# One re-planned step order of a fused attention and feed-forward kernel: weights' mean in fp32 column quarters, factor table by products and two exponentials, tables held once, `w_in` in halves

## The chip, the core and the metric

The kernel runs on one core of a Trainium2 chip. A core has five engines with an instruction stream each: TensorE (PE, matrix products; its weight loads are listed as PEld), VectorE (DVE), ScalarE (ACT), GpSimd (POOL) and SyncE (SP, which here issues most of the DMAs). Every engine works through its own list in order; an instruction whose input is not there holds up all that stand behind it on that engine. The metric is the device time of one execution in microseconds (us). The kernel before takes 166.04 us (median of 2 runs, 165.97 to 166.11).

## The reference

Four batches of eight heads, 768 positions, 64 features. Attention keeps, for each query, the 96 latest keys and the first 8 keys of the sequence, with a bias that falls linearly with the distance. Its result, 3072 tokens by 512 features, goes through a feed-forward block.

```python
scores = scale * q @ k.T + bias                  # bias = -slope[head] * distance
keep = is_global | is_local                      # k < 8, or 0 <= q - k < 96
a = softmax(where(keep, scores, -1e9))
x = (a @ v) as [B*S, H*D]                        # 3072 x 512
h = x @ w_in                                     # 512 -> 1024
solu = h * softmax(h)
mu, var = mean(solu), var(solu)
out = ((solu - mu) / sqrt(var + 1e-6) * g_ln) @ w_out     # 1024 -> 512
```

## The kernel before, in words

**Attention.** Each batch is done in two units of 384 queries. For a unit, `q` and `k` are loaded with the positions in partitions, cast to fp16, turned by TensorE (six products of 128x128 with the identity per pair of heads, L729) and copied out of PSUM as `qT` and `kT` (L269 on ScalarE, L271 on VectorE; all casts and copies of those two engines go through one helper and so have one line). `scores` (L875) are products of key blocks with queries; ScalarE takes their exponential into `eb` (L883). The bias of batch 0 is added in PSUM by products with a table `bw` (L861); batches 1 to 3 take it as a factor, one VectorE multiplication of `eb` by a table `fb` per pair of heads and group (L891, the step `fac`, 24 of them). Column sums are products with ones (L954, L963); their reciprocals are made as exp(-log(sum)): `ln`, a split of the logarithm in two fp16 parts (`lhi` L977, `l` L985), a product that spreads them (L1014) and an exponential into `rr` (L1023). The weighted values are products in two parts: `av1`, then a VectorE copy of one column named `tick` (L1068), for which the second part `av2` waits (both L1058 and L1048). VectorE multiplies the result by `rr` into `xT` (L1083), the turned input of the feed-forward block.

**Feed-forward.** There are 24 tiles of 128 tokens, six to a batch. Per tile: gemm1 (L1117, 16 products of 128x512), an exponential `ef` on ScalarE (L1123), `uu` = h times ef on VectorE (L1126), squares and their sum on ScalarE (L1133) or VectorE (L1137), a turn of `uu` by TensorE or by DMA into `late`'s tiles, gemm2 (L1198, 8 products), and a scaling by the reciprocal deviation into `osb` on ScalarE (L1208) or VectorE (L1211), which is stored. The mean is not taken out of each token: gemm2's weights are centred once instead. The product with `g_ln` (L634, L636, L640) gives `gw_out_sb`, eight products with a matrix of 1/1024 (L647) give the mean over the 1024 rows in every partition, and eight VectorE instructions (L651, named centre here) write g times `w_out` less that mean.

**What sets the order.** All work is cut into some 760 steps. A planner outside the kernel chose the order, and the kernel holds its result as tables: ORDER (the steps' sequence), SLOTS (which buffer each takes), ENGS (the engine, where several could do it) and WARM (products on a constant tile, L1224, that are put in where TensorE would stand). Every engine's list follows from ORDER. The steps' priorities and costs, which the diff also touches, only fed that planner. At most eight loads or stores of SP are under way at a time.

## Time and profile before

| | |
|---|---|
| median of the runs | 166.04 us (165.97 to 166.11) |
| the profiled execution | 166.89 us, of which the span of the profile is 165.2 us |
| TensorE busy | 151.5 us (92%), of it 11.8 us in filler products |
| VectorE / ScalarE / GpSimd busy | 122.5 / 131.7 / 62.4 us |
| first gemm1 of batch 0 starts | 36.95 us |
| first gemm1 of batch 0's second unit starts | 55.37 us |
| first gemm1 of batch 2 starts | 112.64 us |
| last product ends | about 161.5 us |
| moved by DMA | 34.27 MB, mean 207 GB/s |

All times are counted from the span's start. Busy time is a sum over instructions; where it is near the length of a stretch, that engine has hardly stood in it. The profiled execution was 0.85 us longer than the median, so a sum made in its times has to be set against 166.89 us.

### The profile page before, as it was taken

Reading aid. Unit: us, or ns where it says so; the run is one execution under the profiler, and the core shown is the slowest. Engines: PE = TensorE matmul, PEld = TensorE weight load, DVE = VectorE, ACT = ScalarE, POOL = GpSimd, SP = SyncE. Lnnn points to the kernel's source line nnn. Section 1 sums busy time; section 2 is a strip of 40 time slices with the busy share of each in tenths; the row PEclk is TensorE's granted clock in tenths of the full one; section 3 lists DMA queues with packets and bytes.
Section 4 is the critical chain, followed back from the end, with each engine's and each line's share of the span. In section 5 each row is a group of like instructions: output and inputs, shape, how many; then the busy total and the mean of one; then the engine's idle time right before and its main releaser. Section 6 shows DMA issues by size and latency. Waiting matters only on the chain.

```text
span 165.2 us, 4904 instructions
## 1 busy us (share of the span) xinstructions
PE 151.5 (92%) x1936; PEld 83.6 (51%) x1936; DVE 122.5 (74%) x261; ACT 131.7 (80%) x217; POOL 62.4 (38%) x131
## 2 busy tenths in 40 slices
PE   6179988999999889989989999999999999999990
PEld 2046654545666556566545454465445564454550
DVE  6552657898976999997999999678687546758750
ACT  3279999999897987996989999599895775785901
POOL 7849642974312719940993436000205000000000
PEclk9999999999999999999999999999999999999997
DMA  4999999999999779999539999311349338429733
GB/s 146 275 378 293 344 386 322 330 308 321 310 307 278 199 171 294 368 256 248 181 77 211 214 193 210 128 72 63 64 88 122 124 62 201 108 76 108 200 130 129
DMA packets 57879, 34.27 MB, mean 207 GB/s; under 512 B 44920, under 2 KB 53376, under 8 KB 57856
## 3 DMA queue, kind: packets, MB, share of 16 engines
q1 hardware_dynamic: 56704, 31.99, 75.3%
q10 hardware_dynamic: 1152, 1.97, 3.2%
q8 instruction: 15, 0.25, 0.6%
q14 instruction: 8, 0.07, 0.1%
HBM read 23.20 MB, written 6.29 MB: 179 GB/s over the span
## 4 chain that ended last, share of the span: by engine, by line
PE 62%; DVE 13%; ACT 12%; issue 4%; DMA 3%; SPq 2%; POOL 2%; ACTq 0%; DVEq 0%
PE acc L1198 22%; PE acc L1117 20%; PE acc L1058 5%; PE acc L729 4%; ACT eb L883 4%; DVE eb L891 3%; DMA vgn<-in_v_dram 3%; DVE uu L1126 3%; PE acc L1224 3%; PE acc L1014 2%; DVE xT L1083 2%; PE acc L875 2%; ACT x L269 1%; PE acc L1152 1%; ACT gw_out_sb L634 1%
## 5 line engine op out<-in xcount | busy, mean ns | idle before, releaser
L1198 PE MATMUL acc<-gw_out_sb,late 128*128 128x512 f16 (+1 forms) x200 | 45.1, 371 | 0.1
L1117 PE MATMUL acc<-w_in_sb,xT 128*128 128x512 f16 x192 | 44.4, 379 | 0.6 <-DVE uu L1126 0.6
L1126 DVE SCALAR_TENSOR_TENSOR uu<-ef,acc 128x1024 f16<-128x1024 f16 x24 | 29.1, 1217 | 12.0 <-ACT ef L1123 11.7
L1123 ACT ACTIVATE ef<-acc 128x1024 f16<-128x1024 f32 x24 | 24.7, 1028 | 8.6 <-PE acc L1117 8.5
L883 ACT ACTIVATE eb<-acc 128x960 f16<-128x960 f32 (+1 forms) x32 | 29.1, 960 | 2.4 <-PE acc L875 2.4
L1117 PEld LDWEIGHTS <-xT 128*128 128x128 f16 x192 | 18.3, 98 | 21.3 <-issue 1.2
L1198 PEld LDWEIGHTS <-late 128*128 128x128 f16 x200 | 18.7, 98 | 20.1 <-issue 0.6
L729 PE MATMUL acc<-ident,x 128*128 128x128 f16 x192 | 16.5, 234 | 5.0 <-ACT x L269 4.1
L891 DVE TENSOR_TENSOR eb<-eb,fb 128x960 f16<-128x960 f16 (+1 forms) x24 | 18.3, 778 | 0.8 <-ACT eb L883 0.5
L1083 DVE TENSOR_TENSOR xT<-acc,rr 128x384 f16<-128x384 f32 x32 | 16.3, 552 | 2.8 <-ACT rr L1023 1.3
L273 POOL CAST x<-x 128x768 f16<-128x768 f32 x17 | 16.4, 979 | 5.1 <-DMA x<-in_q_dram 2.7
L1133 ACT ACTIVATE sqa<-uu 128x1024 f16<-128x1024 f16 x16 | 16.9, 1059 | 1.6 <-DVE uu L1126 1.5
L729 PEld LDWEIGHTS <-x 128*128 128x128 f16 x192 | 12.9, 104 | 10.3 <-ACT x L269 6.1
L977 POOL TENSOR_SCALAR lhi<-lns,mlo 128x384 f16<-128x384 f32 x5 | 7.1, 1411 | 27.1 <-ACT lns L970 27.1
L1058 PE MATMUL acc<-eb,v 64*64 64x160 f16 (+4 forms) x448 | 16.1, 220 | 0.4 <-DVE tick L1068 0.4
L1058 PEld LDWEIGHTS <-v 64*64 64x64 f16 x448 | 13.2, 106 | 4.4 <-issue 3.2
L1208 ACT ACTIVATE osb<-acc,rstd 128x512 f32<-128x512 f32 (+1 forms) x13 | 8.6, 669 | 7.3 <-PE acc L1198 5.8
L273 POOL CAST v<-v 128x704 f16<-128x704 f32 (+3 forms) x17 | 10.9, 656 | 8.7 <-DMA v<-in_v_dram 4.6
L1023 ACT ACTIVATE rr<-acc 128x768 f32<-128x768 f32 x16 | 12.8, 813 | 0.8 <-PE acc L1014 0.6
L1224 PE MATMUL acc<-busy 128*128 128x512 f16 x31 | 11.8, 494 | 1.5 <-DVE busy L554 1.5
L875 PE MATMUL acc<-qT,kT 64*64 64x160 f16 (+2 forms) x384 | 11.6, 230 | 0.6 <-ACT eb L883 0.5
L1211 DVE TENSOR_SCALAR osb<-acc,rstd 128x512 f32<-128x512 f32 (+1 forms) x12 | 8.7, 725 | 4.0 <-PE acc L1198 2.3
(115 smaller groups left out, 218.5 us busy)
## 6 DMA issues: line engine op xcount, KB each, us to landing
x<-in_q_dram SPq DMA_DIRECT2D x16, 384.0 KB, 5.2
x<-in_k_dram SPq DMA_DIRECT2D x16, 384.0 KB, 6.1
out_dram<-osb SPq DMA_DIRECT2D x16, 256.0 KB, 2.8
v<-in_v_dram SPq DMA_DIRECT2D x12, 192.0 KB, 4.8
w_out<-in_moe_w_out_dram SPq DMA_DIRECT2D x4, 512.0 KB, 6.3
late<-in_moe_w_in_dram SPq DMA_DIRECT2D x4, 512.0 KB, 6.8
v<-in_v_dram SPq DMA_DIRECT2D x12, 160.0 KB, 4.2
out_dram<-osb ACTq DMA_DIRECT2D x7, 256.0 KB, 2.9
```

The lines of the kernel that those rows point to most:

```text
L273: nc.gpsimd.tensor_copy(out=out, in_=in_)
L729: nc.tensor.transpose(out=pt[:, ts(j, P)], in_=a[:, j, ts(pp, P)], identity=ident)
L883: ex["fn"] = (lambda ex=ex, qk=qk, gw=gw: nc.scalar.activation(out=eb[at(qk, "eb")][:, :, 0:gw], in_=big(qk)[:, :, 0:gw], func=AF.Exp, sca ...
L891: nc.vector.tensor_tensor(out=e, in0=e, in1=fb[:, p, :, 0:gw], op=ALU.mult)
L1058: nc.tensor.matmul(out=o_[64 * h : 64 * h + 64, gl : gl + m], lhsT=vv[r, v_at(vi, h, c), pair, :], rhs=view(eb[at(e_own[b, gi, pair], "eb" ...
L1083: nc.vector.tensor_tensor(out=xT[at(xt_own[b], "xT")][:, p, q0:q1], in0=one(av, d)[:, 0:w], in1=rr[at(re, "rr")][:, d, 0:w], op=ALU.mult)
L1117: nc.tensor.matmul(out=ph()[:, ts(fh, 512)], lhsT=xT[at(xt_own[b], "xT")][:, j, ts(t % NA, P)], rhs=w_in_sb[:, j, ts(fh, 512)], start=(j = ...
L1123: ex["fn"] = lambda g1=g1, t=t, ph=ph: nc.scalar.activation(out=ef[at(g1, "ef")], in_=ph(), func=AF.Exp, accum_out=s0[:, t : t + 1])
L1126: u["fn"] = lambda u=u, g1=g1, t=t, ph=ph: nc.vector.scalar_tensor_tensor(out=uu[at(u, "uu")], in0=ef[at(g1, "ef")], scalar=USC, in1=ph(), ...
L1133: nc.scalar.activation(out=sqs_["ACT"], in_=uu[at(u, "uu")], func=AF.Square, accum_out=s2[:, t : t + 1])
L1198: nc.tensor.matmul(out=one(g2)[:, 0:wd], lhsT=uT[at(el_o, "uT")][:, c, :], rhs=gw_out_sb[:, c, sl_], start=(c == 0), stop=(c == NFC - 1))
L1224: nc.tensor.matmul(out=acc[:, spot, :], lhsT=busy16[:, 0:P], rhs=busy16, start=True, stop=True)
```

## The change

**The weights' mean.** The eight multiplications of `w_out` by `g_ln` (three on ScalarE, four on VectorE, one on GpSimd) are gone, and so are the eight fp16 products behind them. Instead `g` is copied 32 columns wide (`gbc`), and eight fp32 products of `gbc` with the loaded `w_out` write four column quarters of one bank, two of them adding up in each quarter (`part_mean`). ScalarE copies the bank to SBUF, and one fp32 product with a constant matrix of 1/32/1024 sums the quarters into the mean. The eight centre instructions stay.

**The factor table.** GpSimd's 16 memsets, its product over 128x1280, its copy over 128x2560 and ScalarE's exponential over 128x1280 are gone. Sixteen products of a 64x64 identity with `bw` put the bias into PSUM, and two exponentials write `fb` from there. Twelve memsets of GpSimd clear the last 32 columns of each `eb` buffer.

**Tables held once.** `bw` and `fb` are one window of 160 columns per pair instead of three side by side; products and `fac` read the window three times with a stride of zero. `fac` always works on 960 columns per partition, where it was 960 or 896.

**`w_in` in halves.** Its four loads were 128 rows of 1024 columns each; now each brings 256 rows of one half of the columns. gemm1 of the first six tiles is two steps, one per half.

**The plan.** ORDER, SLOTS, ENGS and WARM are new throughout. The buffers for loaded `q` and `k` go from six to seven, `uu` from three to four, `rr` from two to three. By the engine table, squares on VectorE go from 8 to 14 of 24, casts of `v` on VectorE from 3 to 6, fillers from 31 to 24.

```diff
 ORDER = """
-11 12 2 161 614 65 139 31 10 6 13 73 3 105 18 123 7 25 4 14 66 16 1 19 86 24 47 0 75 92 5 112 76
+11 12 10 112 139 65 281 19 105 118 2 120 157 7 13 47 0 92 5 295 114 79 15 1 115 14 107 16 25 6 17
...
 WARM = """
-32:0:7 54:0:3 60:0:1 66:0:3 93:4:1 124:2:4 142:4:3 177:5:2 189:5:3 194:5:2 199:7:1 203:7:1
+24:0:5 47:2:0 76:4:1 115:4:1 131:0:6 153:6:3 186:0:1 197:0:5 232:0:1 299:2:1
...
+    def factor_bias(s, d):
+        for par in range(2):
+            for n in range(2):
+                p = 2 * d + n
+                for h in range(2):
+                    o, r = 64 * (h ^ par), slice(64 * h, 64 * h + 64)
+                    nc.tensor.matmul(
+                        out=big(s)[o : o + 64, par, n * WIN : (n + 1) * WIN], lhsT=identb[r, r],
+                        rhs=bw[r, p], start=(n == 0), stop=(n == 1), tile_position=(64 * h, o),
+                        skip_group_check=True)
+
+    def factor_exp(s, d):
+        nc.scalar.activation(
+            out=fb[:, 2 * d : 2 * d + 2].rearrange("r p x n -> r x p n"),
+            in_=big(s)[:, :, 0 : 2 * WIN].rearrange("r x (p n) -> r x p n", n=WIN), func=AF.Exp, scale=inv_sqrt_d)
...
-        for j in range(NCC):
-            _, d = load(lambda i, e, j=j: e.dma_start(
-                out=w32[:, j], in_=moe_w_in.rearrange("(j p) f -> p j f", p=P)[:, j]),
...
+        for fh in range(2):
+            for jj in range(0, NCC, 2):
+                _, d = load(lambda i, e, jj=jj, fh=fh: e.dma_start(
+                    out=w32[:, jj : jj + 2, ts(fh, 512)],
+                    in_=moe_w_in.rearrange("(j p) f -> p j f", p=P)[:, jj : jj + 2, ts(fh, 512)]),
...
-        def mean():
+        pm = step("PE", 1750, 24000, w_out_st + [gb], None, take="one", mode="s", name="part_mean", lat=210, ni=16)
+
+        def parts():
             for j in range(NFC):
-                nc.tensor.matmul(out=one(hold), lhsT=onesm, rhs=gw_out_sb[:, j, :],
-                                 start=(j == 0), stop=(j == NFC - 1))
...
+                x = 32 * (j % 4)
+                nc.tensor.matmul(out=one(pm)[x : x + 32], lhsT=gbc[:, j], rhs=w_out32[:, j],
+                                 start=(j < 4), stop=(j >= 4), tile_position=(0, x), skip_group_check=True)
+        pm["fn"] = parts
+        pc = step(("ACT", "DVE"), (530, 610), 24500, [pm], None, free=[(pm, "one")], lat=(165, 140), name="copy_mean")
+        pc["fn"] = lambda: copy(pc["at"], part, one(pm))
+        wm = step("PE", 870, 25000, [pc, onesm_st, hold], lambda: nc.tensor.matmul(
+            out=one(hold), lhsT=onesq, rhs=part, start=True, stop=True), mode="f", name="mean", lat=210, ni=2)
...
                     def factor(qk=qk, gw=gw, p=p):
-                        e = eb[at(qk, "eb")][:, :, 0:gw]
-                        nc.vector.tensor_tensor(out=e, in0=e, in1=fb[:, p, :, 0:gw], op=ALU.mult)
+                        e = eb[at(qk, "eb")].rearrange("r x (m n) -> r x m n", n=WIN)
+                        f = fb[:, p]
+                        nc.vector.tensor_tensor(
+                            out=e, in0=e, in1=bass.AP(tensor=f.tensor, offset=f.offset,
+                                                      ap=[f.ap[0], f.ap[1], [0, 3], f.ap[2]]),
+                            op=ALU.mult)
...
-        g1 = step("PE", 1728, tt, xt_st[t] + w_in_st, None, take=("big", "ef"), mode="f",
-                  name="gemm1", lat=198, ni=16)
...
+        g1 = step("PE", 864 if early else 1728, tt, xt_st[t] + (w_in_st[:NCC] if early else w_in_st), None,
+                  take=("big", "ef"), mode="f", name="gemm1", lat=198, ni=8 if early else 16)
+        g1e = g1
+        if early:
+            g1e = step("PE", 864, tt + 900, [g1] + w_in_st[NCC:], None, mode="f", name="gemm1b", lat=198, ni=8)
```

What the new tables move is shown at three places. In the changed kernel the lines are L602 for `w_in`'s loads, L613 for `w_out`'s, L634 for centre, L871 for `fac`, L1066 for `xT`, L1117 for `uu`, L1128 for squares, L1202 for `osb`, L1051 for `tick` and L273 for VectorE's casts and copies.

The first place is SP's list around `w_in` and the last loads of `w_out`; `x` are loads of `q` and `k`. Before:

```order
L621 DMA w_out_70<-in_moe_w_out_dram 128x2x512 x2
L611 DMA late<-in_moe_w_in_dram 128x1024
L481 DMA x_5_105<-in_q_dram 128x2x384
L495 DMA v_0_110<-in_v_dram 128x3x64 x2
L503 DMA vt_88<-in_v_dram 64x4x64
L510 DMA vgn<-in_v_dram 64x1x64
L611 DMA late<-in_moe_w_in_dram 128x1024 x3
```

Of the change:

```order
L602 DMA late<-in_moe_w_in_dram 128x2x512
L485 DMA v_2_115<-in_v_dram 128x3x64
L485 DMA v_2_115<-in_v_dram 128x2x64
L613 DMA w_out_72<-in_moe_w_out_dram 128x2x512
L602 DMA late<-in_moe_w_in_dram 128x2x512 x3
```

The last load of `w_out` has moved behind the first of `w_in`. Of the four loads of `w_in`, the two with the second half of the columns stand first, and the two with the first half, for which gemm1's first step waits, come last.

The second place is VectorE's list from the first `xT` to the `xT` of batch 0's second unit. Before, five of the centre instructions stand ahead of the first `xT`, and these rows lead on from the last two of the eight:

```order
L891 TENSOR_TENSOR eb_139<-eb_139,fb 128x2x448
L891 TENSOR_TENSOR eb_140<-eb_140,fb 128x960
L1126 SCALAR_TENSOR_TENSOR uu_150,s_92<-ef_148,acc 128x1024
L271 COPY kT_118<-acc 128x768
L1126 SCALAR_TENSOR_TENSOR uu_151,s_92<-ef_149,acc 128x1024
L271 CAST x_3_109<-x_2_102 128x768
```

Of the change:

```order
L1066 TENSOR_TENSOR xT_100<-acc,rr_150 128x384 x2
L871 TENSOR_TENSOR eb_141<-eb_141,fb 128x960
L273 CAST w_in_sb<-late 128x512
L634 SCALAR_TENSOR_TENSOR gw_out_sb<-w_out_72,g_74,acc 128x512 x8
L1117 SCALAR_TENSOR_TENSOR uu_154,s_94<-ef_152,acc 128x1024
L871 TENSOR_TENSOR eb_142<-eb_142,fb 128x960
L1128 SCALAR_TENSOR_TENSOR sqv,s_95<-uu_154 128x1024
L1117 SCALAR_TENSOR_TENSOR uu_155,s_94<-ef_153,acc 128x1024
```

All eight centre instructions now stand in one piece behind the first unit's `xT` and ahead of the first `uu`, and a square that ScalarE did has joined VectorE's list. From the first centre to the second unit's last `xT`, VectorE's list holds: the 8 centres, 3 `uu`, 2 squares, 2 `fac`, one copy each of `qT`, `kT` and `late`, two small casts of `v`, the four rows of a statistics group, one `osb`, 2 `tick` and 4 `xT`.

The third place is VectorE's list between the second unit's `xT` and the first `xT` of batch 2, at its start. Before:

```order
L271 CAST x_3_109<-x_2_102 128x768
L891 TENSOR_TENSOR eb_131<-eb_131,fb 128x960
L271 CAST v_1_114<-v_0_110 128x11x64
L891 TENSOR_TENSOR eb_133<-eb_133,fb 128x960
L891 TENSOR_TENSOR eb_134<-eb_134,fb 128x2x448
L891 TENSOR_TENSOR eb_132<-eb_132,fb 128x2x448
L1126 SCALAR_TENSOR_TENSOR uu_150,s_92<-ef_149,acc 128x1024
```

Of the change:

```order
L273 CAST x_2_111<-x_5_107 128x768
L273 CAST x_3_112<-x_2_104 128x768
L273 CAST x_0_109<-x_1_103 128x768
L871 TENSOR_TENSOR eb_136<-eb_136,fb 128x960
L871 TENSOR_TENSOR eb_135<-eb_135,fb 128x960
L273 COPY qT_127<-acc 128x768
L871 TENSOR_TENSOR eb_133<-eb_133,fb 128x960
L273 COPY qT_125<-acc 128x768
L1117 SCALAR_TENSOR_TENSOR uu_157,s_94<-ef_153,acc 128x1024
```

Two casts and two copies have come in ahead of the first `uu`, and one `fac` has gone. Over the whole stretch the list holds, before and with the change: `fac` 15 and 12, squares 5 and 7, casts of `x` 3 and 5, casts of `v` 1 and 3, copies of `qT` and `kT` 4 and 5, `lhi` 2 and 1, `l` 2 and 1, `osb` 1 and 3, statistics groups 3 and 2; 12 `xT`, 9 `uu`, 6 `tick` and one copy of `late` in both. TensorE's list holds, between that first `xT` of batch 2 and batch 2's first gemm1, one gemm2, one product group of L1014 and one turning of `q` fewer than before, and two scores more; behind that gemm1 it holds the same groups as before, 12 gemm1 and 13 gemm2 among them.

157 lines of the change are left out of this document (62 added, 95 removed), and 93 rows, old and new, of tables (ENGS, ORDER, SLOTS).

## The prediction

> **What bounds the kernel now.** First the page's busy times, to see which engine could set the span at all.
>
> ```profile
> span 165.2 us, 4904 instructions
> PE 151.5 (92%) x1936; PEld 83.6 (51%) x1936; DVE 122.5 (74%) x261; ACT 131.7 (80%) x217; POOL 62.4 (38%) x131
> ```
>
> An average of 92% hides stages with different limits. So the span is cut where the dependences cut it: at the first gemm1 (36.95), the first gemm1 of batch 0's second unit (55.37), the first of batch 1 (79.68), the first of batch 2 (112.64) and the end of the products. The columns are the stretch's length, then busy time and instructions of PE, PEld, DVE, ACT and POOL, the granted clock, the DMA share and GB/s.
>
> ```profile
> 0.00:36.95 36.95, 29.79 (x424) 16.35 (x425) 23.52 (x67) 29.08 (x40) 24.72 (x82) 1.00 1.01 309
> 36.95:55.37 18.42, 17.88 (x252) 11.04 (x251) 14.82 (x30) 16.85 (x30) 5.67 (x13) 1.00 1.05 302
> 55.37:79.68 24.31, 23.02 (x392) 14.28 (x389) 22.86 (x42) 21.30 (x34) 14.14 (x18) 1.00 0.95 253
> 79.68:112.64 32.96, 32.02 (x471) 17.61 (x467) 29.38 (x56) 29.59 (x50) 14.42 (x17) 1.00 0.74 161
> 112.64:161.50 48.86, 48.82 (x412) 24.36 (x408) 31.93 (x71) 34.37 (x66) 3.41 (x3) 1.00 0.53 110
> ```
>
> From 112.64 TensorE stands for 0.04 us in all: whatever delays batch 2's first gemm1 delays the end by as much, and nothing behind it matters. In 36.95 to 112.64 TensorE stands for 75.69 − 72.92 (the three rows' sum) = 2.77 us: that is all a better order can win there. The first 36.95 us are not TensorE's own, though it looks busy; the fillers alone (line L1224) show it:
>
> ```profile
> 0.00:36.95 36.95, 11.63 (x31) 3.21 (x31) 1.00 1.01 309
> ```
>
> Useful there are 29.79 − 11.63 = 18.2 us. The DMA engines are full, and ScalarE ends the wait: the last cast of `w_in` on it ends as the first gemm1 starts.
>
> ```profile
> 36.28 0.61 ACT L269 CAST w_in_sb<-late 128x512 f16<-128x512 f32 x1
> ```
>
> The engine to watch behind that is VectorE. From the `xT` of batch 0's second unit to the first `xT` of batch 2:
>
> ```profile
> 52.91:103.19 50.28, 47.56 (x737) 27.86 (x728) 47.74 (x87) 45.31 (x75) 29.31 (x35) 1.00 0.93 220
> ```
>
> It is busy 47.74 of 50.28 us, 95%, and the chain that ended last runs through it there:
>
> ```profile
> 57.43 2.24 DVE eb L891 x3
> 59.67 1.15 DVE uu L1126 x2
> ```
>
> It has 2.5 us to spare in 50. A plan that gives it more work there has to find the room.
>
> **The change part by part.** The sum is made from the profiled execution's span, whose execution took 166.89 us, 0.85 above the median of 166.04; a difference found in it is set on the median.
>
> *Repeated tables.* `fac` now reads `fb` three times over. The nearest row is VectorE's own repeated read, 1280 columns in 483 ns, against the present `fac`:
>
> ```profile
> L271 DVE COPY bw<-bw 128x1280 f16<-128x1280 f16 x1 | 0.5, 483 | 0.0
> L891 DVE TENSOR_TENSOR eb<-eb,fb x24: 610/651/1459, 27.8 to 114.3; 128x960 f16<-128x960 f16 x12, 128x896 f16<-128x896 f16 x12
> L1083 DVE TENSOR_TENSOR xT<-acc,rr x32: 546/550/559, 33.8 to 137.7; 128x384 f16<-128x384 f32 x32
> ```
>
> The repeat cost that copy no pace, so I take none for `fac`; above, its slow value, 1459. That spread, beside `xT`'s 2%, means `fac` is stretched by something else. By the Trainium skill, "SBUF — State Buffer", section "SBUF: two separate sides", a GpSimd instruction and a VectorE one with two SBUF inputs shut each other out; `fac` (two) against `xT` (one) agrees with it. By that rule GpSimd's lost table work would help only where `fac` runs, and it went from the head.
>
> *Weights' mean.* These go, or are replaced:
>
> ```profile
> L647 PE MATMUL acc<-gw_out_sb,onesm 128*128 128x512 f16 x8 | 1.9, 379 | 0.0
> L640 DVE TENSOR_SCALAR gw_out_sb<-w_out,g 128x512 f16<-128x512 f32 x4 | 2.8, 739 | 0.6 <-DMA w_out<-in_moe_w_out_dram 0.6
> L634 ACT ACTIVATE gw_out_sb<-w_out,g 128x512 f16<-128x512 f32 x3 | 2.1, 733 | 0.8 <-DMA vgn<-in_v_dram 0.8
> L651 DVE SCALAR_TENSOR_TENSOR gw_out_sb<-w_out,g,acc 128x512 f16<-128x512 f32 x8 | 5.6, 742 | 0.5 <-PE acc L647 0.5
> ```
>
> VectorE loses 2.8 and ScalarE 2.1 us, ahead of the first gemm1. No trace here shows an fp32 product of this size. Below, four quarters could run beside each other like the four 32-column products of L927, whose group is hardly longer than one of them:
>
> ```profile
> 23.84 0.35 PE L927 MATMUL acc<-qT,kg 128*32 128x384 f16 x4
> L927 PE MATMUL acc<-qT,kg 128*32 128x384 f16 x32 | 2.6, 335 | 0.6 <-DVE kT L271 0.6
> 37.12 3.45 PE acc L1117 x16
> ```
>
> At the fp16 pace of gemm1, 3.45 / 16 = 0.216 us a product, two rounds would take 0.43. Above: fp32 numbers taken as two halves make four products of each, and eight in a row take, as an estimate from that pace, 8 × 4 × 0.216 = 6.9. I take quarters side by side with four products each, 2 × 4 × 0.216 = 1.75, and 4 × 0.216 = 0.87 for the last product. The Trainium skill, "FP8 and Floating Point Precision", section "TensorE Precision Notes", counts four passes for true FP32, and "TensorEngine Tiling (Array Packing)", section "Key Properties", lets different tiles work in parallel but says that a change of tiling mode drains TensorE; L927 bears out the parallel tiles, no run here shows the passes, and by these rules the two steps give the same 1.75 and 0.87 plus two drains of unknown length.
>
> The mean's products stood ahead of the first spread (L1014) before; now they stand behind `av2`, whose last row is the first here, and the copy through ScalarE follows:
>
> ```profile
> 33.83 0.45 PE L1058 MATMUL acc<-eb,v 64*64 64x160 f16 x7
> 30.02 2.72 DVE L651 SCALAR_TENSOR_TENSOR gw_out_sb<-w_out,g,acc 128x512 f16<-128x512 f32 x4 [0.46 <-PE acc L647]
> 52.91 1.95 DVE L1083 TENSOR_TENSOR xT<-acc,rr 128x384 f16<-128x384 f32 x4 [0.54 <-PE acc L1058]
> ```
>
> If `av2` ends where it did, at 34.3, the centres can start at 34.3 + 1.75 + 0.7 + 0.9 = 37.6; if the 2.1 us off ScalarE and the mean's 1.9 out of spread's way pull it forward in full, at 33.6. I take 36.0, past the middle, because more bytes lie ahead (below); before, the first started at 30.02 and five were done ahead of the first `xT`. VectorE's prices, from its groups between 52.91 and 103.19:
>
> ```profile
> L1126 DVE SCALAR_TENSOR_TENSOR uu<-ef,acc 128x1024 f16<-128x1024 f16 x9 | 10.8, 1213 | 0.4 <-issue 0.3 <-ACT ef L1123 0.2
> L1137 DVE SCALAR_TENSOR_TENSOR sqv<-uu 128x1024 f16<-128x1024 f16 x5 | 6.7, 1350 | 0.1
> L891 DVE TENSOR_TENSOR eb<-eb,fb 128x960 f16<-128x960 f16 x7 | 6.5, 935 | 0.1
> L891 DVE TENSOR_TENSOR eb<-eb,fb 128x896 f16<-128x896 f16 x8 | 6.2, 785 | 0.1
> L271 DVE COPY kT<-acc 128x768 f16<-128x768 f16 x4 | 3.7, 954 | 0.3 <-POOL v L273 0.3
> L271 DVE CAST x<-x 128x768 f16<-128x768 f32 x3 | 2.4, 797 | 0.0
> L977 DVE TENSOR_SCALAR lhi<-lns,mlo 128x384 f16<-128x384 f32 x2 | 1.3, 666 | 0.0
> L985 DVE TENSOR_TENSOR l<-lns,lhi 128x384 f16<-128x384 f32 x2 | 1.1, 546 | 0.0
> L271 DVE CAST v<-v 128x704 f16<-128x704 f32 x1 | 0.9, 875 | 0.0
> L1172 DVE SCALAR_TENSOR_TENSOR va<-s,va 128x3 f32<-128x3 f32 x3 | 1.1, 355 | 0.2
> L1211 DVE TENSOR_SCALAR osb<-acc,rstd 128x512 f32<-128x512 f32 x1 | 0.7, 736 | 0.0
> ```
>
> From 36.0 VectorE has, in a row: 8 centres at 2.72 / 4 = 0.68, 5.4; 3 `uu` at 1.21, 3.6; 2 squares at 1.35, 2.7; 2 `fac` at 0.65, 1.3; three copies at 0.95, 0.95 and 0.68, 2.6; casts of `v` 0.35; a statistics group of four rows up to 0.36, 0.9; `osb` 0.75; ticks 0.3; 4 `xT` 1.95. That is 19.9, and ends at 55.9 where it ended at 52.91 + 1.95 = 54.86: **+1.0** (−1.4 to +2.6) at the second unit. ScalarE's gain is swallowed there, since `uu` stands behind all eight centres.
>
> *`w_in` in halves, loads.* The half that gemm1's first step needs lands last, so splitting gives nothing by itself. Ahead of the last `w_in` load stand 10196 KB instead of 9732, counted from the two lists by the page's sizes: 464 KB, 1.5 us at the 309 GB/s of the first window. The same bytes in `w_out`'s shape land sooner:
>
> ```profile
> w_out<-in_moe_w_out_dram SPq DMA_DIRECT2D x4, 512.0 KB, 6.3
> late<-in_moe_w_in_dram SPq DMA_DIRECT2D x4, 512.0 KB, 6.8
> ```
>
> Between 0 and 0.5 each comes off, up to 2.0; I take the two as even. ScalarE then casts up to 0.7 sooner, which counts only in the rival below.
>
> *Factor table.* GpSimd loses these two, and ScalarE an exponential of 1.3, for two exponentials of about 0.6:
>
> ```profile
> L316 POOL TENSOR_TENSOR fx<-dm,sf 128x1280 f32<-128x1280 f32 x1 | 2.3, 2318 | 0.0
> L328 POOL COPY fb<-fb 128x2560 f16<-128x2560 f16 x1 | 2.3, 2317 | 0.1
> ```
>
> Nobody waited for them, and the new small products (about 0.4) replace fillers in the first 10 us: 0 to −0.5, taken as 0. The cover is the loads; without it the 0.4 would count.
>
> *The stretch 52.91 to 103.19.* By the prices above and the counts shown with the change: squares +2 with their readout, 2.9; casts of `x` +2, 1.6; of `v` +2, 1.75; a copy, 0.95; `osb` +2, 1.5; `lhi`, `l` and a statistics group less, −0.7 − 0.55 − 0.9; `fac` from 12.7 to 12 of 0.85 to 0.935, −2.5 to −1.5. That is +4.0 to +5.0: 51.7 to 52.7 us of work in a stretch of 50.28. It takes 51.7 if VectorE never stands and 52.7 / 0.95 = 55.5 if it stands as now. I take 52.2 / 0.975 = 53.6: **+3.3** (+1.5 to +5.2). Against it, between that `xT` and batch 2's gemm1 TensorE has one gemm2 (1.73) less, and L1014 and a turning less against two more scores come out even: **−1.7**. Behind that gemm1 the work is the same.
>
> The sum: 1.0 + 3.3 − 1.7 = +2.6, the profiled 166.89 to 169.5, the median to **168.6**; from the ends, −1.4 + 1.5 − 1.7 and 2.6 + 5.2 − 1.7, 164.4 to 172.1.
>
> **The rivals.** *VectorE keeps up.* TensorE alone binds, gemm1 starts up to 0.7 sooner by ScalarE's relief, and of the 2.77 us of standing some goes: 166.04 − 0.7 − 0.7 = 164.6, at most −0.7 − 2.77, 162.6. For it speaks that four `uu` and three `rr` buffers loosen the order; against it the 95%.
>
> *The fp32 quarters run one after the other.* Slower: `part_mean` takes 6.9, 5.1 more, and the centres start at 41.1; VectorE's list has no room until the second unit's gemm1, so all of it lands: 173.7. It decides once the quarters' end passes the landing of `w_in`, some 2 us above the value taken. The parallel L927 speaks against it.
>
> *The repeat costs `fac` its pace.* At twice 0.65, 12 in the stretch and 2 ahead: 14 × 0.65 = 9.1 less the spare 1.3, 176. The copy of `bw` speaks against it.
>
> *The change does not do what it says* in one part: the halves of `w_in`, counted above at nothing.
>
> **How the numbers follow.** VectorE takes over 0.55 (164.4 to 172.1; 0.30 of it below 169.4), VectorE keeps up 0.29, quarters in a row 0.10, `fac` loses pace 0.06. A measurement of this kernel can tell about 2% from no change, 162.7 to 169.4. Faster: 0.05, from the second case's best end. Same: 0.30 + 0.24 = 0.54. Slower: 0.25 + 0.10 + 0.06 = 0.41. The range, 163.6 to 172.6, leaves out the quarters' and `fac`'s cases and the second case's best end, about 0.2.
>
> **What would show it.** Right: the second unit's first gemm1 at 56 to 57, VectorE over 97% busy from there to batch 2's first `xT`, TensorE standing 4 to 6 us between its first and 13th gemm1 where it was 2.77, `part_mean` near 1.75. Wrong: the 13th gemm1 before 112.6, `fac` far under 0.78 in the mean since less of GpSimd runs beside it, or `av` so early that the centres start at 33.

## The result

The changed kernel takes 171.85 us (median of 2 runs, 170.98 and 172.73) against 166.04: 1.033 times the time before (95% interval 1.028 to 1.039), **slower by 5.8 us**. The prediction said 168.6 in a range of 163.6 to 172.6: the measured time is inside it and on the forecast side of no change, but the forecast has less than half of the loss, and it held "same" (0.54) likelier than "slower" (0.41). A run more than 1.5% above the fastest of the same kernel is left out of the ratios below, so the kernel with `w_in`'s loads in another order, of whose four runs one remains, has none.

The page of the changed kernel, busy times (profiled execution 172.73 us, the longer of its two runs, against 166.89 before):

```profile
span 170.7 us, 4929 instructions
PE 154.7 (91%) x1955; PEld 84.0 (49%) x1955; DVE 131.6 (77%) x275; ACT 125.0 (73%) x206; POOL 53.7 (31%) x116
```

The span of the changed kernel, cut at the same five events (columns as in the prediction):

```profile
0.00:37.54 37.54, 30.23 (x422) 16.99 (x422) 23.91 (x64) 27.07 (x38) 16.64 (x73) 0.95 0.96 301
37.54:57.44 19.90, 18.69 (x253) 10.52 (x252) 17.61 (x36) 15.38 (x27) 7.10 (x9) 1.00 1.00 280
57.44:85.69 28.25, 24.91 (x442) 15.30 (x434) 25.57 (x43) 23.71 (x37) 17.65 (x22) 1.00 0.94 245
85.69:118.34 32.65, 32.09 (x447) 17.10 (x441) 31.61 (x65) 25.41 (x43) 7.59 (x10) 1.00 0.67 135
118.34:167.33 48.99, 48.80 (x408) 24.09 (x407) 32.92 (x72) 32.98 (x63) 4.69 (x4) 1.00 0.53 116
```

Held against the rows before, the five stretches are longer by 0.6, 1.5, 3.9, −0.3 and 0.1 us. So 5.7 of the 5.84 us are there when the 13th gemm1 starts (118.34 for 112.64), and two thirds arose between the second unit's first gemm1 and that of batch 1. That stage does not hold quite the same work: TensorE has 442 products in it instead of 392, 44 of the 50 more being scores, and is busy 1.9 us longer, while the stage behind it holds 24 fewer. Between the first gemm1 and the 13th TensorE is busy 75.69 us instead of 72.92 (+2.8) and stands 5.1 us instead of 2.8 (+2.3). In what follows, "the stretch" without more is this one: 75.7 us before, 80.8 after.

Where it shows is the chain of waits. Before, from the product of L1014 that spreads the first logarithms of batch 1 to that batch's `xT`:

```profile
73.95 0.36 PE acc L1014 x4
...
74.66 1.83 PE acc L1198 x8
...
76.83 0.16 PE acc L1014 x4
...
78.78 0.71 ACT rr L1023
...
79.52 0.56 DVE xT L1083
```

And after, the same place (the spread is L997, gemm2 L1189, `osb` on ScalarE L1199):

```profile
74.94 0.38 PE acc L997 x4
...
77.59 2.61 DMA out_dram<-osb
80.20 0.68 ACT osb L1199
80.88 2.10 ACT rr L1006 x3
...
83.85 0.40 DVE xT L1066
```

The first of these spreads is only 1.0 us late (74.94 for 73.95). From there to batch 1's first gemm1 it takes 79.68 − 73.95 = 5.7 us before and 85.69 − 74.94 = 10.8 after. TensorE's timeline of the changed kernel has two gemm2 between the first spread and the others where one stood before, and ScalarE's has an `osb` that waits for a store to free its buffer ahead of three `rr`:

```profile
76.53 3.63 PE L1189 MATMUL acc<-gw_out_sb,late 128*128 128x512 f16 x16
80.08 0.52 PE L997 MATMUL acc<-l,onesr 64*64 64x384 f16 x8
```

```profile
80.19 0.69 ACT L1199 ACTIVATE osb<-acc,rstd 128x512 f32<-128x512 f32 x1 [0.99 <-DMA out_dram<-osb]
80.78 2.20 ACT L1006 ACTIVATE rr<-acc 128x768 f32<-128x768 f32 x3
```

### The profile page after: what moved, and what is told of

The parts are those of the page before. It is cut to its first block, busy times and chain, and to the rows that moved or that the text cites. A ratio compares the mean times of both kernels' runs of the same rounds, so it can differ in the third digit from the quotient of the medians.

```text
span 170.7 us, 4929 instructions
## 1 busy us (share of the span) xinstructions
PE 154.7 (91%) x1955; PEld 84.0 (49%) x1955; DVE 131.6 (77%) x275; ACT 125.0 (73%) x206; POOL 53.7 (31%) x116
## 4 chain that ended last, share of the span: by engine, by line
PE 49%; DMA 15%; ACT 12%; DVE 10%; SPq 4%; POOL 4%; issue 3%; POOLq 0%; ACTq 0%; DVEq 0%
PE acc L1189 21%; PE acc L1104 17%; DMA late<-in_moe_w_in_dram 5%; DMA v<-in_v_dram 5%; DMA x<-in_q_dram 4%; ACT eb L862 4%; PE acc L1041 3%; SPq L471 2%; DVE eb L871 2%; ACT ef L1114 2%; ACT rr L1006 2%; PE acc L712 2%; DVE x L273 2%; DMA out_dram<-osb 2%; PE acc L854 2%
## 5 line engine op out<-in xcount | busy, mean ns | idle before, releaser
L1104 PE MATMUL acc<-w_in_sb,xT 128*128 128x512 f16 x192 | 45.3, 379 | 1.5 <-DVE uu L1117 0.7
L1189 PE MATMUL acc<-gw_out_sb,late 128*128 128x512 f16 (+1 forms) x200 | 44.5, 371 | 0.0
L1117 DVE SCALAR_TENSOR_TENSOR uu<-ef,acc 128x1024 f16<-128x1024 f16 x24 | 29.1, 1215 | 6.9 <-ACT ef L1114 6.8
L862 ACT ACTIVATE eb<-acc 128x896 f16<-128x896 f32 (+1 forms) x32 | 29.3, 951 | 3.0 <-PE acc L854 2.9
L1189 PEld LDWEIGHTS <-late 128*128 128x128 f16 x200 | 18.7, 98 | 21.1 <-DMA late<-uu 0.5
L712 PE MATMUL acc<-ident,x 128*128 128x128 f16 x192 | 17.7, 240 | 2.9 <-POOL x L275 1.2
L1066 DVE TENSOR_TENSOR xT<-acc,rr 128x384 f16<-128x384 f32 x32 | 16.4, 550 | 3.0 <-ACT rr L1006 1.9
L1128 DVE SCALAR_TENSOR_TENSOR sqv<-uu 128x1024 f16<-128x1024 f16 x14 | 17.8, 1268 | 0.1
L871 DVE TENSOR_TENSOR eb<-eb,fb 128x960 f16<-128x960 f16 x24 | 17.3, 735 | 0.6 <-ACT eb L862 0.6
L275 POOL CAST x<-x 128x768 f16<-128x768 f32 x14 | 12.6, 901 | 13.4 <-DMA x<-in_q_dram 6.6
L1199 ACT ACTIVATE osb<-acc,rstd 128x512 f32<-128x512 f32 (+1 forms) x14 | 9.1, 654 | 7.2 <-PE acc L1189 4.8
L854 PE MATMUL acc<-qT,kT 64*64 64x160 f16 (+2 forms) x384 | 13.7, 237 | 0.7 <-ACT rr L1006 0.3
L271 ACT CAST x<-x 128x768 f16<-128x768 f32 x9 | 7.5, 837 | 5.2 <-DMA x<-in_k_dram 3.2
L1124 ACT ACTIVATE sqa<-uu 128x1024 f16<-128x1024 f16 x10 | 10.5, 1052 | 0.9 <-DVE uu L1117 0.9
L854 PEld LDWEIGHTS <-kT 64*64 64x64 f16 x384 | 9.6, 111 | 3.1 <-issue 2.0
```

Of the source, the lines that this page charges most:

```text
L712: nc.tensor.transpose(out=pt[:, ts(j, P)], in_=a[:, j, ts(pp, P)], identity=ident)
L854: nc.tensor.matmul(out=sc[o : o + 64, par, col : col + n], lhsT=kk[r, BLK * c : BLK * c + BLK], rhs=qq[r, g0 : g0 + n], start=fresh, stop= ...
L862: ex["fn"] = (lambda ex=ex, qk=qk, gw=gw: nc.scalar.activation(out=eb[at(qk, "eb")][:, :, 0:gw], in_=big(qk)[:, :, 0:gw], func=AF.Exp, sca ...
L871: nc.vector.tensor_tensor(out=e, in0=e, in1=bass.AP(tensor=f.tensor, offset=f.offset, ap=[f.ap[0], f.ap[1], [0, 3], f.ap[2]]), op=ALU.mult)
L1066: nc.vector.tensor_tensor(out=xT[at(xt_own[b], "xT")][:, p, q0:q1], in0=one(av, d)[:, 0:w], in1=rr[at(re, "rr")][:, d, 0:w], op=ALU.mult)
L1104: nc.tensor.matmul(out=ph()[:, ts(fh, 512)], lhsT=xT[at(xt_own[b], "xT")][:, j, ts(t % NA, P)], rhs=w_in_sb[:, j, ts(fh, 512)], start=(j = ...
```

## The experiments

The edits of the tables are given by the steps that they move, since the rows of numbers tell nothing. `u` is the step of `uu`, `sq` a square; a number behind `#` names the step of its kind. The "stretch" figures are from each kernel's own profile, cut at the same events.

### The parts without the new order

Two kernels with the order and engines of before: one with all four parts of the change, one with all but the new mean.

```diff
 # order, engines and buffers of before; the code of the changed kernel
-gw#0..7, mean (8 fp16 products)
+part_mean, copy_mean (ScalarE), mean (fp32), in the old mean's place
+c_fbias#0..1 and c_fac#0..1 among the first turns
```

> All four parts of the change (mean in fp32 quarters, factor table by products, tables held once, w_in in halves with the first half loaded first), but the order, the engine of each step and the buffers as the kernel before has them. Theory O, that the new order and engine table cost the 5.8 us and the parts cost nothing: 164.5 to 167 us. Theory P, that the parts themselves cost (the fp32 mean comes late, the halves and the repeated tables cost TensorE and VectorE time): 169 us or more.

> Three parts of the change (factor table by products and two exponentials, tables held once, w_in in halves) with the mean, the order and the engines of the kernel before. If the 3.5 to 4.4 us by which the first gemm1 came late in the two runs of all parts were the mean's longer path, as their traces say (ScalarE or TensorE stood for the quarters): first gemm1 at 36.5 to 37.5 and 165 to 167 us. If the repeated tables, the halves or the small products cost something too: 168 us or more.

All four parts: 169.85 us, 1.021 (1.013 to 1.028). Without the mean: 168.2 us, 1.012 (1.006 to 1.019). The stretch takes 75.3 and 75.9 us, as before (75.7), and the loss lies ahead of it: the first gemm1 starts at 40.41 and 39.68 instead of 36.95 (the second figure from that kernel's longest run, 169.61, with a granted clock of 0.87 in the head). So **behind the first gemm1 the parts cost nothing in these two kernels**, the table read three times among them. In the head they cost here what the forecast gave no price for. Two of TensorE's waits in the head of the kernel with all parts:

```profile
PE acc L997 <- ACT eb L862: 2.2, 1, 2.2
...
PE acc L712 <- ACT fb L320: 0.8, 1, 0.8
```

The kernel before has neither of the two; its wait for the casts of `x`, 4.1 us in all, is as long there as here and no part of the loss. ScalarE is late by then: it holds the table's two exponentials, and it stood 1.6 us for the quarters' products before it could copy them. Since in these two kernels the places in the head are mine, two other placings were tried.

```diff
 # the same parts and the old order, first other placing
-turn_k#4, part_mean; copy_mean on ScalarE; four centres ahead of tick, the others among and behind the xT
+part_mean, turn_k#4; copy_mean on VectorE; one centre ahead of tick, 7 in one piece behind the last xT
```

> All four parts again in the order and with the engines of the kernel before, with the new steps placed so that nothing stands for them: the copy of the quarters on VectorE, where it has room, the products of the factor table ahead of two exponentials that take the place of two multiplications by g on ScalarE, seven of the centres behind the first unit's xT. Theory O (order costs, parts are free): the first gemm1 back at 36.5 to 37.5 where parts_old_order had 40.4, the stages behind it as long as before, 165 to 167 us. Theory P: the first gemm1 at 38.5 or later, or longer stages, 168 us or more.

```diff
 # second other placing
+turn_k#4, part_mean, ..., turn_q#4, mean; copy_mean on VectorE; 5 centres behind the last xT, 2 behind the first u
```

> All four parts in the order and with the engines of the kernel before, once more with other places in the first 37 us: the products of the factor table in a bank that no filler waits for, the quarters' copy on VectorE behind the first unit's logarithm, the fp32 sum of the quarters behind the next turning, five centres behind the first unit's xT and two behind the first uu. In parts_old_order, parts_old_order2 and old_mean_old_order the stages behind the first gemm1 were as long as before to 0.4 us (but for the second's first stage), and only the head was longer. If it was my places there: first gemm1 at 36.5 to 38 and 165 to 167 us. If the parts cost the head something wherever they stand: 39 or later, 168 us or more.

171.64 us, 1.034 (1.029 to 1.038), and 169.62 us, 1.017 (1.012 to 1.022). In the first the head takes 41.33 us and the stretch 76.7, since the first `uu` stands behind the seven centres. In the second the head takes 38.06 and the stretch 78.0: TensorE stands behind the first gemm1, for a bank that the mean holds until the last centre has read it, and for `uu`:

```profile
PE acc L712 <- DVE gw_out_sb L634: 1.9, 1, 1.9
PE acc L1143 <- DVE uu L1117: 0.5, 1, 0.5
```

In three placings the parts cost 2.8 to 5.6 us in the old order (0.017 and 0.034 of 166.04). None was free, but all three are my own places in a finished order, so whether the parts have a price of their own in the head stays open. What is shown is that the table's products and exponentials and the mean's longer path find no slack there by themselves. The stage from the second unit's first gemm1 to batch 1's takes 23.5 to 24.3 us in all four of these kernels, as before (24.31). The stage ahead of it, 18.4 in the first two as before, takes 20.2 and 20.8 in the two that have seven centres behind the first unit's `xT`; the change has all eight there and 19.9.

### VectorE's load

Does the work that the new table gives VectorE explain the stretch? Once in the old order, by giving VectorE as many squares as the change does:

```diff
 # the kernel before; ENGS
-sq#1, 3, 11, 6, 8, 14: ScalarE
+sq#1, 3, 11, 6, 8, 14: VectorE
```

> The kernel before with six more squares on VectorE (14 of 24, as the change has), its order unchanged; 7.8 us come on VectorE, five of the six between its first gemm1 and batch 2's, and 7.5 us go off ScalarE. Theory V: VectorE's 2.5 us of room there are used up, so 168 to 170 us. Theory W: 165.5 to 167.5 us.

172.34 us, 1.039 (1.034 to 1.044): **in the old order six squares alone cost as much as the whole change**. VectorE's busy time in the stretch goes from 67.1 to 73.2 us and the stretch from 75.7 to 80.5; the change takes VectorE to 74.8 and the stretch to 80.8. Its longest stage, from batch 1's first gemm1 to batch 2's, took 35.33 us instead of 32.96:

```profile
82.61:117.94 35.33, 32.46 (x470) 17.73 (x467) 32.87 (x62) 26.93 (x44) 14.98 (x17) 1.00 0.70 155
```

VectorE does 32.87 us of work there, where it did 29.38, and TensorE stands for 2.9 us where it stood for 0.9.

Then in the new order, by taking work off VectorE:

```diff
 # the changed kernel; ENGS
-sq#0, 2, 3, 6, 8, 11: VectorE
+sq#0, 2, 3, 6, 8, 11: ScalarE
```

> The changed kernel with six of its fourteen squares on VectorE given back to ScalarE (8 on VectorE as before), the order unchanged. Theory V, that VectorE's list is what binds between the first gemm1 and batch 2's first: two squares of 1.3 us go ahead of the second unit's xT and three or four behind it, so 167.5 to 170 us. Rival theory W, that waits of TensorE on several engines, set by the order, cost the time whoever does the squares: 171 to 174 us, since ScalarE gets 6 times 1.25 us more.

```diff
 # the changed kernel; ENGS
-cast_q#11, 12, 14, 15, cast_k#10, cast_v#14, 17, 19: VectorE
+cast_q#11, 12, 14, 15, cast_k#10, cast_v#14, 17, 19: GpSimd
```

> The changed kernel with five casts of q and k and three of v given from VectorE to GpSimd, which is busy for 17.7 of 28.3 and 7.6 of 32.7 us in the two stages; 6.7 us go off VectorE between the second unit's xT and batch 2's, and none comes on ScalarE. Theory V (VectorE's load binds, 25.6 of 28.3 and 31.6 of 32.7 us busy): 167.5 to 169.5 us. Theory W (the order's waits cost the time whoever does the work): 171 to 173 us.

Both together:

> The changed kernel with both six squares on ScalarE and eight casts on GpSimd: 14 us off VectorE, which then has as little to do as before. If VectorE's load is what the new order loses by (as it is for the old order with six more squares, 172.3 us): 166 to 169 us. If the new order loses by its own waits and by what it adds on TensorE (75.7 us busy against 72.9 between the first gemm1 and batch 2's): 170 us or more.

172.67 us, 1.037 (1.029 to 1.045); 170.97 us, 1.028 (1.020 to 1.036); 172.97 us, 1.034 (1.025 to 1.043). VectorE's busy time in the stretch falls to 66.3, 69.1 and 62.5 us, below that of before in two of the three, and the stretch stays at 80.5, 80.1 and 82.2 (the last with a granted clock of 0.92 in its first stage). The squares bring ScalarE to 70.2 us there, above the 67.7 of before; the casts leave it at 64.3. With the casts on GpSimd, the stage from the second unit's first gemm1 to batch 1's:

```profile
56.06:83.59 27.53, 24.14 (x443) 15.02 (x435) 21.45 (x40) 23.18 (x37) 19.26 (x24) 1.00 1.01 258
```

VectorE works 21.45 us in it, less than before (22.86), and the stage takes 27.53 us instead of 24.31. So more work on VectorE is enough to cost 5 us, but it is not what holds the new order: once relieved, it waits for the others. The reading "VectorE binds, so relieve it" falls.

### The halves, the loads' order, and the two gemm2

```diff
 # the changed kernel; order of SP's list
-w_out#3 behind the first load of w_in; columns 512 to 1023 first
+w_out#3 ahead of it; columns 0 to 511 first
```

> The changed kernel with the last load of w_out ahead of w_in's loads and w_in's first half of the columns loaded first. If the centres and uu bind the second unit (theory V), the first gemm1 comes about 1 us sooner and the mean some 1 us sooner, and the end by 0.5 to 1.5: 170 to 171.5 us. If the head is bound by loads alone, as much as 2.5 us sooner, 169.3; if the mean waits for av2 alone, no change, 171.9.

```diff
 # the changed kernel; TensorE's list, tiles 0 to 5
-gemm1, ..., gemm1b
+gemm1, gemm1b in one piece
```

> The changed kernel with the second half of gemm1 directly behind the first in each of the first six tiles. The trace has 23.2 us of gemm1 between TensorE's first gemm1 and batch 2's first, against 22.7 before, and two ef come up to 2 us sooner. If TensorE's own time matters there: 0.5 to 1.5 us less, 170.4 to 171.4. If VectorE binds (theory V): no change or up to 0.5 us less, 171.4 to 171.9.

The first came to 174.05 us, with no ratio; its fastest run, the profiled one, took 170.87 us, with the first gemm1 at 37.05 and a stretch of 79.3. The second: 172.24 us, 1.035 (1.027 to 1.043). Neither the order of these loads nor the splitting of gemm1 shows as a loss: no run of the two is more than 0.2 us below the faster run of the change (170.98).

Next, the pair of gemm2 that the chain showed between the spreads:

```diff
 # the changed kernel; TensorE's list ahead of batch 1
-gemm2#5, gemm2#3, spread, ..., scores#22
+spread, ..., scores#22, gemm2#5, gemm2#3   (their osb and stores behind as well)
```

> The changed kernel with two gemm2 (and their osb) moved on TensorE from ahead of the spreads of batch 1's first unit to just ahead of batch 1's first gemm1. In the trace that spread waits for them from 76.5 to 80.1, and VectorE then stands 2.5 us until 84. Theory W (the second stage is long by the order of TensorE's list): the stage from the second unit's first gemm1 to batch 1's falls from 28.2 to 25 to 26.5 us, of which the end keeps 1 to 3: 169 to 171 us. Theory V (VectorE is what binds there): the stage stays at 27.5 or more, 171.5 us.

The same with the eight casts on GpSimd:

> The same and the eight casts of casts_gpsimd on GpSimd too. If both causes are at work one behind the other, the gains add up: 167.5 to 169.5 us. If either alone binds, the time of the better of the two, 170 us or more.

174.72 us, 1.048 (1.042 to 1.054), and 172.72 us, 1.035 (1.026 to 1.044): slower than or like the change, and the stage between the second unit's first gemm1 and batch 1's grew from 28.3 to 31.5 and 30.3 us. The granted clock was 0.89 in that stage both times, so how much of the growth is the order's is not known; but another run of the second kernel, at a clock of 1.00, took 173.0 us. The end of the stage in the second of them:

```profile
82.20 3.58 PE acc L1189 x16
85.78 0.43 PE acc L1104 x2
```

The pair now stands right ahead of gemm1. Moving what the chain named brought nothing back, so it was at most the place of the loss and not its cause.

### Two scores steps

The old order has 12 scores steps ahead of the first gemm1, the new one 10; so 22 instead of 20 lie between it and the 13th, where TensorE has little slack. The group of all scores products in the stretch, before and after:

```profile
L875 PE MATMUL acc<-qT,kT 64*64 64x160 f16 (+2 forms) x240 | 7.0, 228 | 0.6 <-ACT eb L883 0.5
```

```profile
L854 PE MATMUL acc<-qT,kT 64*64 64x160 f16 (+2 forms) x264 | 9.2, 229 | 0.7 <-ACT rr L1006 0.3 <-DVE xT L1066 0.3
```

That is 2.2 of TensorE's 2.8 us. So the two steps were taken back in the new order, moved alone in the old order, and taken back with VectorE relieved too.

```diff
 # scores_early: the changed kernel
+scores#12, scores#8 behind mean, exp#12, exp#8 behind ScalarE's last cast of w_in
-gemm1#1, scores#12, gemm1b#1, scores#8
+gemm1#1, gemm1b#1
 # load, cast, turn and copy of q#4 change places with those of k#14; six fillers fewer
 # scores_late: the kernel before
-scores#12, scores#8, ..., gemm1#1, gemm1#2
+gemm1#1, gemm1#2, scores#12, scores#8   (exp#12, exp#8, fac#4, fac#0 with them; three fillers fewer)
```

> The changed kernel, but the two scores steps that its order has behind the first gemm1 and the order before had ahead of it (the last two groups of batch 0's second unit) stand ahead of the first gemm1 again, with their exponentials; for that the load, cast, turn and copy of the q they need change places with those of a k needed later. Theory T (TensorE, which never has time to spare behind the first gemm1, got 2.2 us of scores more there: 264 rows of scores for 9.2 us against 240 for 7.0): the 13th gemm1 comes about 2.2 us sooner behind the first one (78.6 us instead of 80.8), the time is 169 to 170.3. Theory W (waits between the engines set by the new order, whatever TensorE has to do): the 80.8 stays within 0.8 and the time is 171 or more.

> The kernel before, but the same two scores steps, their exponentials and the two table multiplications that need them stand behind the first two gemm1, as in the changed kernel; nothing else is moved. Theory T: the stretch from the first to the 13th gemm1 grows from 75.7 to about 77.9; against it ScalarE has 1.9 us less ahead of the first gemm1, which may bring that up to 0.7 sooner: 167.2 to 168.5. Theory W: that stretch grows by under 0.8, and the time is 165.3 to 166.9.

> As the changed kernel with the two scores steps ahead of the first gemm1, and six of VectorE's squares given to ScalarE besides. If TensorE's added work and VectorE's load bind in turn, so that taking either away alone shows nothing, both together give 167 to 169. If T alone holds, about as with the scores steps alone, 169 to 170.3. If W holds, 171 or more.

172.7 us, 1.034 (1.027 to 1.042); 168.11 us, 1.011 (1.007 to 1.015); 174.55 us, 1.044 (1.037 to 1.051). The first and the third took back nothing. In the old order the move made the stretch 1.2 us longer (76.9) and the head as much shorter (35.75), with the 13th gemm1 at 112.67 as before. The groups in the scores_early and the scores_late kernel:

```profile
L854 PE MATMUL acc<-qT,kT 64*64 64x160 f16 (+1 forms) x240 | 8.4, 229 | 1.0 <-ACT rr L1006 0.3 <-DVE uu L1117 0.3 <-DVE xT L1066 0.3
```

```profile
L875 PE MATMUL acc<-qT,kT 64*64 64x160 f16 (+2 forms) x264 | 7.7, 228 | 0.6 <-ACT eb L883 0.5
```

Two scores steps have a price of 0.7 us (7.7 − 7.0), not 2.2. The same 240 products take 7.0 us busy in the old order and 8.4 in the new, each as long as before (228 and 229 ns): they overlap less. TensorE's greater busy time is thus for the most part not more work. In the old order theory T is not refuted: 168.11 us lies in its range, and the 1.2 us lie between what the two theories gave. For the loss of the change it falls, since taking the steps back brought nothing.

### The loads

The last suspect: engines that wait for loads. In the changed kernel the chain goes through a `v` load that lands 7.78 us after it is issued and holds ScalarE, and GpSimd stands for loads:

```profile
39.29 7.78 DMA v<-in_v_dram
...
47.30 1.11 ACT ef L1114 x2
```

```diff
 # in both kernels; they leave out bytes that the result needs, and measure time only
-load_heads(..., 2 * p0, 2 * npr, lo, run)
+load_heads(..., 2 * p0, 2 * npr // cut, lo, run)       # cut = 2 from the 7th load of q and of k on
-load_v(..., b, p, h, lo, hi)
+load_v(..., b, p, h, lo, hi if b == 0 else lo + 1)
```

> The kernel before with the same loads cut in the same way. It stood for 2.8 us between the first and the 13th gemm1, little of it for loads: by both theories that stretch stays between 74.5 and 75.9, the first gemm1 comes as before, since nearly the same bytes lie ahead of it, and the time is 164.5 to 166.5. It is what the cut kernel with the change is to be held against.

> The changed kernel with the same instructions, but 20 of the 32 loads of q and k (all that batch 0's first needs do not touch) bring one of their two heads, and the loads of v for batches 1 to 3 one block of 64 columns; the rest of the buffers keeps what an earlier load left, so the values are not the reference's. Theory D (the new order has engines wait for loads: in its chain of waits DMA holds 15% where it held 3%, and the q/k and v casts on ScalarE, VectorE and GpSimd stand for loads behind the first gemm1): the stretch from the first to the 13th gemm1 falls from 80.8 to 75.5 to 77.5, no more than 1.5 above that of the kernel before with the same loads cut, and the time to 164.5 to 167.5. Theory E (the engines' own lists): that stretch stays above 79 and the time above 169.

> The changed kernel with the same loads cut, and six of VectorE's squares given to ScalarE besides. Theory D with VectorE next in line: 1 to 3 us faster than with the loads cut alone. D alone: within 1 us of it. Theory E: 169 or more, as the squares alone changed nothing.

Before with the loads cut: 166.27 us, 0.998 (0.996 to 1.001). The change with the loads cut: 170.96 us, 1.028 (1.022 to 1.033). With squares on ScalarE besides: 172.85 us, 1.038 (1.030 to 1.046). The three stages of the stretch, before with the loads cut and after with the loads cut:

```profile
37.20:55.61 18.41, 17.88 (x252) 11.04 (x251) 15.24 (x30) 16.83 (x30) 6.43 (x14) 1.00 0.60 166
55.61:79.03 23.42, 22.67 (x391) 13.96 (x389) 21.95 (x42) 21.05 (x34) 12.55 (x16) 1.00 0.49 134
79.03:111.98 32.95, 32.06 (x470) 17.67 (x467) 29.43 (x56) 29.55 (x50) 14.72 (x17) 1.00 0.50 116
```

```profile
36.86:56.51 19.65, 18.77 (x253) 10.53 (x252) 19.00 (x37) 15.43 (x28) 8.86 (x10) 1.00 0.51 146
56.51:83.51 27.00, 24.42 (x442) 15.19 (x435) 23.28 (x42) 23.41 (x37) 15.11 (x20) 1.00 0.46 131
83.51:116.54 33.03, 32.28 (x447) 17.16 (x441) 32.08 (x65) 25.42 (x43) 7.02 (x10) 1.00 0.45 98
```

DMA is half idle in both, and the stretch still differs by 79.7 − 74.8 = 4.9 us. In the changed kernel with the loads cut VectorE and ScalarE stand for no load any more behind the first gemm1, and GpSimd for 6.1 us instead of 16.5 (waits of 0.2 us and more). Theory D falls: **the loss is in the lists of the engines themselves**. The first gemm1 starts at 36.86 instead of 37.54. But in the two kernels with the gemm2 moved, whose lists in the head are the change's own, it starts at 36.11 and 38.47, so where the 0.6 us of the head come from is not shown. VectorE is 97% busy in the first and the third stage (19.00 of 19.65, 32.08 of 33.03) but 86% in the second (23.28 of 27.00), which holds 3.6 of the 4.9 us.

## Why the prediction missed

The prediction's sum was 1.0 + 3.3 − 1.7 = +2.6 at the 13th gemm1. The three terms measured +2.1, +3.0 and +0.6, together 5.7; behind it +0.1.

**The mean: right in its sizes.** The quarters' products, their sum and the centres in the timelines of TensorE and VectorE:

```profile
32.22 1.92 PE L626 MATMUL acc<-w_out,gbc 128*32 128x512 f32 x16 [0.37 <-ACT eb L862]
34.85 1.12 PE L631 MATMUL acc<-part,onesq 128*128 128x512 f32 x2
36.01 5.36 DVE L634 SCALAR_TENSOR_TENSOR gw_out_sb<-w_out,g,acc 128x512 f16<-128x512 f32 x8 [0.68 <-PE acc L631]
```

1.92 us for 1.75, 1.12 for 0.87, and the centres from 36.01, where 36.0 was taken. That this start was met so closely is luck: `av2` ended at 31.85, 2.4 us sooner than before, of the up to 4.0 that the forecast allowed, but from there it took 4.2 us and not 3.35; and in the kernels with the same lists in the head the centres start anywhere between 35.2 and 37.5. The 1.92 us also end the rival of quarters one after the other, which had 6.9 us there.

**The second unit: +1.0 taken, +2.1 measured.** The prediction priced VectorE's works from the centres on back to back, 19.9 us. They took 20.97 (36.01 to 56.98), because VectorE stood three times:

```profile
47.31 0.62 DVE L273 CAST v<-v 128x192 f16<-128x192 f32 x2 [0.94 <-DMA v<-in_v_dram]
...
53.47 0.75 DVE L1202 TENSOR_SCALAR osb<-acc,rstd 128x512 f32<-128x512 f32 x1 [0.51 <-ACT rstd L1172]
54.81 0.16 DVE L1051 COPY tick<-acc 128x1 f32<-128x1 f32 x1 [0.59 <-PE acc L1041]
55.03 1.95 DVE L1066 TENSOR_TENSOR xT<-acc,rr 128x384 f16<-128x384 f32 x4
```

That is 2.04 us; the works themselves were 1.0 shorter than priced (a square 1.2, not 1.35). With the loads cut the second unit's first gemm1 came at 56.51, 0.9 sooner; 0.5 of that is there already at the first centre (35.53), and the first and the last of the three waits are gone.

**`w_in`'s loads: taken as even, slower in this order.** A load of half the columns landed 9.2 us after its issue (median of four), where whole rows took 6.8. That is not shown to be the shape's: the same halves took 6.6 us in the kernel with all parts in the old order. The first gemm1 waited for GpSimd's cast of it. It came 0.6 us late, which VectorE, at the centres until 41.4, didn't feel:

```profile
late<-in_moe_w_in_dram SPq DMA_DIRECT2D x4, 512.0 KB, 9.2
```

```profile
36.87 0.61 POOL L275 CAST w_in_sb<-late 128x512 f16<-128x512 f32 x1 [2.65 <-DMA late<-in_moe_w_in_dram]
```

**The stretch from that `xT` to batch 2's: +3.3 taken, +3.0 measured.** It took 53.28 us instead of 50.28:

```profile
55.03:108.31 53.28, 49.83 (x732) 28.14 (x725) 50.31 (x89) 44.03 (x70) 25.79 (x32) 1.00 0.90 201
```

```profile
L871 DVE TENSOR_TENSOR eb<-eb,fb x24: 641/650/1351, 32.2 to 120.0; 128x960 f16<-128x960 f16 x24
```

VectorE holds 50.31 us, against 52.2 by the sum, and is 94% busy, not 97.5: two errors that nearly cancel, and the experiments say that VectorE's load is not what binds here. So the size came out right by luck, and the reason is only half right: in the old order such a load is worth 4.8 us, in the new one taking it away is worth nothing. `fac` with its repeated read takes 650 ns in the median (651 before), as the prediction took it; the rival with twice that is out.

**The step that failed: "between that `xT` and batch 2's gemm1 TensorE has one gemm2 (1.73) less ... −1.7".** It makes 2.3 of the 3.1 us by which the sum was short. TensorE took 10.03 us there, where it took 9.45, before and after:

```profile
103.19:112.64 9.45, 9.45 (x199) 5.62 (x197) 6.96 (x15) 7.52 (x11) 0.00 (x0) 1.00 0.32 116
```

```profile
108.31:118.34 10.03, 9.47 (x213) 5.61 (x212) 9.28 (x25) 6.70 (x11) 0.00 (x0) 1.00 0.38 124
```

It is busy as long as before, 9.47 for 9.45 us. The groups of products in this piece of the two traces show why, before and after:

```profile
L1198 PE MATMUL acc<-gw_out_sb,late 128*128 128x512 f16 x22 | 5.3, 380 | 0.0
L875 PE MATMUL acc<-qT,kT 64*64 64x160 f16 (+2 forms) x60 | 2.0, 228 | 0.0
```

```profile
L1189 PE MATMUL acc<-gw_out_sb,late 128*128 128x512 f16 x19 | 4.6, 380 | 0.0
L854 PE MATMUL acc<-qT,kT 64*64 64x160 f16 (+2 forms) x84 | 2.9, 227 | 0.0
L839 PE MATMUL acc<-bw,identb 64*64 64x64 f16 x8 | 0.9, 203 | 0.5 <-ACT eb L862 0.5
```

When VectorE starts that `xT`, TensorE is not at the same place of its list: three products of gemm2 fewer are left, not eight, and the two scores steps take 0.9 + 0.4 us and a wait of 0.5 for an exponential. The credit was counted between two places in a list, but TensorE lags or leads the engine whose event marks the place. Between its first and its 13th gemm1 it does the same products in both kernels, except two scores steps with their bias and one filler more and one turning of six products fewer; no credit of a whole gemm2 was to be had.

**The rivals.** VectorE keeps up: out. Of the change not doing what it says, the halves of `w_in`: joining gemm1's two steps brought nothing back; loads of whole rows in the new order were not run. Of the signs set down, the second unit's gemm1 (56 to 57 against 57.44) was missed by 0.4, VectorE's 97% by 3 points, and TensorE's standing of 4 to 6 us came out at 5.1. Of the signs against it, the 13th gemm1 was not early, and `fac`'s mean is 735 ns, where it was 778.

**What stays open.** Shown: the stage from the second unit's first gemm1 to batch 1's is as long as before in all four kernels with the parts alone (at most 24.3 us), and 26.6 to 31.5 us with the new plan, so at least 2.3 of its 3.9 us come with the plan. With the new plan the stretch is 3.6 us longer or more in all kernels tried, whatever was taken away (squares, casts, both; the split of gemm1; the place of two gemm2; two scores steps; about two fifths of the bytes moved). What in the plan costs this time (order, engines, buffers or fillers) could not be isolated. Not told apart are the 1.5 us of the stage ahead of it: seven centres behind the first unit's `xT` made it 1.8 and 2.4 us longer in the old order too, so they may be the price of the later mean. Not shown either is whether the parts would be free in the head if an order were made for them. No version with the change beat the kernel before.

## What to carry to other kernels

Price a new order by the engine that never stands: list all that it does between the first and the last event that matter, in both versions, and give credit for nothing that is merely counted between two places of its list. An engine that is 95% busy costs time as soon as it gets more work (six squares, 6 us), but relieving the same engine in another order may bring nothing: in the changed kernel TensorE's waits in the stretch are spread over VectorE, ScalarE and GpSimd, none longer than 0.9 us. Test both directions. Try the parts of a change in the old order first: here that told that the longest piece of the loss was the plan's and not the arithmetic's.

## What was not expected of the hardware

An fp32 product of 128x512 stands in the trace as two rows of 0.6 us, so the eight products of the quarters as sixteen:

```profile
L626 PE MATMUL acc<-w_out,gbc x16: 592/592/617, 32.2 to 33.6; 128*32 128x512 f32 x16
```

Sixteen rows of 592 ns in 1.92 us are 4.9 beside each other on average, where the 16 rows of 379 ns of two gemm1 in 3.45 us are 1.8 (a gemm1 is 8 products, 192 rows for 24 tiles, and not 16 as the description of the kernel has it): the quarters do run side by side in fp32. The Trainium skill, "FP8 and Floating Point Precision", section "TensorE Precision Notes", counts four passes for true FP32. The trace agrees roughly in time, though it shows two rows a product and not four: four passes at gemm1's 0.216 us are an estimated 0.87, and the single product took 1.12 us from its first start to its last end, where a row of gemm1 too is longer (379 ns) than its pace.

Loads whose bytes are cut by so much that the DMA share in the first two stages of the stretch falls from 1.05 and 0.95 to 0.60 and 0.49 left the time of the kernel before as it was (0.998, 0.996 to 1.001): the nearly full DMA engines behind the first gemm1 did not limit it by a measurable amount.
